# The first load of a decode attention kernel comes in two pieces: 16 rows, then 112

## The chip, the core and the metric

The kernel runs on one core of a Trainium2 chip. The metric is the device time of one execution in microseconds; less is better. The figures given for the kernel before are the median of three runs and one execution taken with the hardware profiler.

## What is computed

One decode step of a block with grouped-query attention over a long cache, gated by a small dense network. There are two sequences (B = 2) with one new token each, 32 query heads, 8 key/value heads, a cache of 32,768 positions, heads of 128, a model width of 512, and everything is float32. Cut to what matters:

```python
xn = layernorm(x)                                  # x: (2, 1, 512)
q  = (xn @ wq) split into 32 heads                 # wq: 512 x 4096
s  = softmax(q . k_cache / sqrt(128)) . v_cache    # both caches: 2 x 8 x 32768 x 128
s  = s @ wo                                        # wo: 4096 x 512
h  = relu(xn @ w1 + b1)**2                         # w1: 512 x 1792
g  = silu(h @ w2 + b2)                             # w2: 1792 x 512
return x + s * g
```

The two caches are 537 MB of the 561 MB that the kernel reads; each byte is used once.

## The kernel before

The host packs the inputs so that each load is a rectangle of 128 rows (one for each partition of the on-chip memory) with long contiguous rows. There are three large buffers of 128 x 64 KiB: `kslot`, `vslot` and `wbuf`. The sixteen pairs of a sequence and a key/value head are each cut in two halves of 16,384 positions, which makes 32 turns (`NT`). A turn takes one load of keys (`kt`, 8 MiB, into `kslot`) and one of values (`vt`, 8 MiB, into `vslot`).

All large loads are issued from SP, in an order written out by hand. At the head there are three, with nothing to wait for:

- L85: `wm`, the weights of the dense network (w1 and w2), 128 rows of 57,344 bytes, into the first 28/32 of `vslot`; it signals `gv`
- L87: `wq`, 128 rows of 65,536 bytes, into `wbuf`; it signals `wq_sem`
- L88: the first keys into `kslot`; it signals `gs`

Two small loads with x and the biases (`xr`, 16 KB, L126, and `x16`, 4 KB, L128) are issued from ACT.

Then PE makes three passes with one and the same body, `pe_values` (64 matmuls in the trace, two for each of the 32 in the code, L364: rows of `vslot` against the columns of `pT`), before the turns begin. The first multiplies by w1 and the second by w2, both out of `vslot`; the third is the product with wq, which ACT and DVE copy from `wbuf` into `vslot` (L200, L206, L209). Each pass starts when the semaphore `gv` has reached a count, 17 for each pass; 16 of the first 17 come from the load of `wm` and one from DVE:

```python
    dve.wait(t_pad)                                    # L164
    v.tensor_copy(pT[:, 0:128]..., xs[...]).then_inc(gv, 1)   # L165, L166
```

Ahead of these lines DVE makes the layer norm of x out of the small load (from L139) and fills the rest of `pT` (L163). The empty columns of `vslot` above `WM` are set to zero by GpSimd; `t_pad` stands for this. After the first pass, DVE goes on at L182 with what PE has turned (L374).

After the third pass SP issues the first load of values (L227, `vslot`). From there on each buffer is loaded again as soon as PE has used it: SP waits for the scores of a turn (L347) and issues the next keys (L237), then for its values (L364) and issues the next values (L240; the last one in two parts, L242 and L243). Once the turns are over, `wo` is loaded in seven pieces (`sp_last`, L326), and the last products, the gate and the sum with x follow (L392 to L432), then one store of 64 KB (L434). At the end SP clears all the semaphores used in one range (L435, L436).

Of the kernel before, what the change touches and what calls it, by code (L numbers as in the profile page):

```python
# [14 lines left out]
P = 128  # L15
# [13 lines left out]
WM = 28 * W  # L29
# [26 lines left out]
def build(nc, xr, x16, kt, vt, wq, wm, wo, out):  # L56
    pe, act, dve, pool, sp = (Engine(nc, e, n) for e, n in (
        (nc.tensor, "pe"), (nc.scalar, "act"), (nc.vector, "dve"), (nc.gpsimd, "pool"), (nc.sync, "sp")))
# [3 lines left out]
    def sb(name, *shape):  # L62
        return nc.alloc_sbuf_tensor(name, [P, *shape], F32)

    kslot, vslot, wbuf = sb("kslot", SLOT), sb("vslot", SLOT), sb("wbuf", SLOT)
# [3 lines left out]
    xb, gate, yb, gpad = sb("xb", P), sb("gate", P), sb("yb", P), sb("gpad", P)  # L69
# [10 lines left out]

    gv, ge, gb, gc, gd, gs, dm, ex, os, vh = (nc.alloc_semaphore(n) for n in ("gv", "ge", "gb", "gc", "gd", "gs", "dm", "ex", "os", "vh"))
    tail_sem = [nc.alloc_semaphore(f"tail{i}") for i in range(len(TAIL))]
    wq_sem, xr_sem, xb_sem, wx_sem, out_sem = (nc.alloc_semaphore(n) for n in ("wq", "xr", "xb", "wx", "out"))

    nc.sync.dma_start(vslot[:, 0:WM], wm[:, 0:WM]).then_inc(gv, 16)  # L85
    nc.sync.sem_clear(out_sem)
    nc.sync.dma_start(wbuf[:, :], wq).then_inc(wq_sem, 16)  # L87
    nc.sync.dma_start(kslot[:, :], kt[0, 0]).then_inc(gs, 16)  # L88
# [30 lines left out]
    t_pad = pool.done(g.memset(vslot[:, WM:], 0.0))  # L119
# [41 lines left out]
        t_x = dve.done(v.tensor_copy(xs[32 * q:32 * q + 32, :, :], xq[:, q, :, 0:8]))  # L161
    dve.wait(t_x, t_pT)
    v.tensor_copy(pT[:, 0:256].rearrange("p (d q z) -> p d q z", d=ND, q=4)[:, :, 0:3, 0:B], xs[:, :, None, 0:B].to_broadcast([P, ND, 3, B])).then_inc(gs, 17 * (PRO - 1) + 1)  # L163
    dve.wait(t_pad)  # L164
    v.tensor_copy(pT[:, 0:128].rearrange("p (h z) -> p h z", h=2)[:, :, 48:52].rearrange("p h (e b) -> p h e b", e=2),  # L165
                  xs[:, :, 0:B].rearrange("p (h e) b -> p h e b", h=2)).then_inc(gv, 1)  # L166

# [264 lines left out]
    t = dve.done(v.tensor_add(xb[:, :], yb[:, :], xb[:, :]))  # L432
    sp.wait(t)
    nc.sync.dma_start(out, xb[:, :]).then_inc(out_sem, 16)  # L434
    used = sorted(x.num for x in [e.sem for e in (pe, act, dve, pool, sp)] + [gv, ge, gb, gc, gd, gs, dm, ex, os, vh] + tail_sem + [wq_sem, xr_sem, xb_sem, wx_sem])  # L435
    nc.sync.sem_clear(range(used[0], used[-1] + 1))  # L436
    nc.sync.wait_ge(out_sem, 16)

# [44 lines left out]
```

## Time and profile before

| | us |
|---|---|
| median of the runs | 1302.14 |
| lowest and highest of the runs | 1302.06, 1302.2 |
| span of the profiled execution, first to last instruction | 1300.8 |
| PE busy | 691.4 |
| DVE busy | 86.0 |
| ACT busy | 99.1 |
| mean rate of the DMA engines over the span | 431 GB/s |

The profiled execution has no time of its own apart from its span, which is 1.34 us below the median of the runs; the difference lies before the first and after the last instruction. A row of the timeline or of the chain begins with the start in us from the beginning of the span and with the duration or the busy time of the group; `L85` is line 85 of the kernel; `x64` a count of instructions; and what stands in brackets is the idle time of the engine before, and what ended it. `SPq` and `ACTq` mark the instructions that issue transfers from those two engines; a row of them tells how long the issue took, not the transfer. In a list of transfers the last number of a row is the median time in us from issue to landing.

### The profile page before, as it was taken

To read this page: it belongs to the slowest core of one execution; us is meant where nothing else is said; L and a number is where in the kernel's file an instruction comes from. 1 tells how busy PE (TensorE), PEld (TensorE's weight loads), DVE (VectorE), ACT (ScalarE), POOL (GpSimd) and SP (SyncE) were. 2 spreads that over 40 slices of the span, in tenths; PEclk is the share of its full clock that TensorE was granted. 3 is DMA by queue.
4 is the path that set the end of the run, shared out by engine and by line. 5 is a ranking of instruction groups with operands and counts; after the bars stand their busy time and mean duration, and the time that the engine had idled before them with its cause. 6 is when DMAs were issued, how large, how long until landed. Compare 5 with 4: busy or idle time off the path is not lost.

```text
span 1300.8 us, 11201 instructions
## 1 busy us (share of the span) xinstructions
PE 691.4 (53%) x4781; PEld 189.5 (15%) x4781; DVE 86.0 (7%) x366; ACT 99.1 (8%) x202; POOL 5.7 (0%) x22
## 2 busy tenths in 40 slices
PE   3746546545545545645544644654554554554557
PEld 0111111111111111111111111111111111111112
DVE  2100000000000000000000000000000000000001
ACT  0301001010010001001010100001001000100100
POOL 1000000000000000000000000000000000000000
PEclk9877677677778677767767767767767767776878
DMA  9999999999999999999999999999999999999998
GB/s 420 419 451 419 447 423 429 441 419 451 419 451 419 451 419 431 439 419 451 419 451 419 451 419 431 439 419 451 419 451 419 451 419 431 439 419 451 419 435 373
DMA packets 10840, 561.08 MB, mean 431 GB/s; under 512 B 1216, under 2 KB 1368, under 8 KB 1752
## 3 DMA queue, kind: packets, MB, share of 16 engines
q1 hardware_dynamic: 10800, 561.06, 99.8%
q10 hardware_dynamic: 40, 0.02, 0.0%
HBM read 561.01 MB, written 0.07 MB: 431 GB/s over the span
## 4 chain that ended last, share of the span: by engine, by line
DMA 74%; PE 24%; issue 1%; DVE 0%; POOL 0%; SPq 0%; POOLq 0%
DMA vslot<-in_vt 70%; PE o_ps L364 24%; DMA wbuf<-in_wo 3%; DMA vslot<-in_wm 1%; PE wb L392 0%; DVE vslot L209 0%; DVE vslot L206 0%; PE acc L422 0%; POOL pT L197 0%; POOL pT L179 0%; SPq L243 0%; PE acc L426 0%; SPq L242 0%; DVE yb L430 0%; DVE xb L432 0%
## 5 line engine op out<-in xcount | busy, mean ns | idle before, releaser
L364 PE MATMUL o_ps<-vslot,pT 128*16 128x512 f32 x2304 | 327.6, 732 | 225.7 <-DMA vslot<-in_vt 201.5
L347 PE MATMUL sc<-kslot,qz 128*32 128x512 f32 x2048 | 294.1, 739 | 277.1 <-DMA kslot<-in_kt 277.1
L347 PEld LDWEIGHTS sc<-kslot,qz 128*32 128x32 f32 x2048 | 71.2, 132 | 478.5 <-DMA kslot<-in_kt 284.7
L364 PEld LDWEIGHTS o_ps<-vslot,pT 128*16 128x16 f32 x2304 | 69.6, 112 | 454.6 <-issue 223.5
L309 ACT ACTIVATE prob<-sc,nm 128x512 f32<-128x512 f32 x32 | 22.0, 687 | 633.9 <-DVE nm L277 633.9
L270 DVE TENSOR_REDUCE r<-sc 128x1 f32<-128x512 f32 x32 | 22.1, 692 | 557.7 <-PE sc L347 557.7
L318 ACT COPY o_sb<-o_ps 128x512 f32<-128x512 f32 x32 | 18.8, 586 | 480.2 <-PE o_ps L364 480.2
L353 PE MATMUL tp<-ident,prob 128*128 128x128 f32 x128 | 25.6, 333 | 50.7 <-ACT prob L309 50.7
L291 DVE TENSOR_REDUCE t<-ot 128x4 f32<-128x64 f32 x32 | 7.2, 225 | 547.6 <-PE ot L374 547.6
L374 PE MATMUL ot<-ident,o_sb 128*128 128x128 f32 x140 | 23.0, 287 | 25.0 <-ACT o_sb L318 22.9
L353 PEld LDWEIGHTS tp<-ident,prob 128*128 128x128 f32 x128 | 16.4, 164 | 56.8 <-ACT prob L309 56.8
L350 PE MATMUL ms<-ident,r 128*128 128x128 f32 x32 | 10.3, 323 | 26.4 <-DVE r L270 26.4
L374 PEld LDWEIGHTS ot<-ident,o_sb 128*128 128x128 f32 x140 | 14.7, 140 | 57.3 <-ACT o_sb L318 52.4
L311 ACT COPY pT<-tp 128x512 f32<-128x512 f32 x32 | 18.8, 586 | 28.4 <-PE tp L353 28.4
L309 ACT ACT_TABLE_LOAD x16 | 20.5, 1283 | 0.3
L350 PEld LDWEIGHTS ms<-ident,r 128*128 128x128 f32 x32 | 4.2, 133 | 55.4 <-DVE r L270 55.4
L355 PEld LDWEIGHTS ms<-selh,l 128*128 128x128 f32 x64 | 12.1, 236 | 0.0
L355 PE MATMUL ms<-selh,l 128*128 128x4 f32 x64 | 10.5, 235 | 0.0
L273 DVE TENSOR_REDUCE mh<-ms 128x4 f32<-128x128 f32 x32 | 9.3, 292 | 10.9 <-PE ms L350 10.9
L200 ACT COPY vslot<-wbuf 128x4096 f32<-128x4096 f32 x2 | 7.1, 3610 | 0.0
L309 ACT ACTIVATION_READ_ACCUMULATOR prob<-sc,nm 128x1 f32 x32 | 6.2, 192 | 0.0
L392 PE MATMUL wb<-wbuf,oX 128*16 128x512 f32 x24 | 4.4, 900 | 2.2 <-DMA wbuf<-in_wo 2.2
(86 smaller groups left out, 78.0 us busy)
## 6 DMA issues: line engine op xcount, KB each, us to landing
vslot<-in_vt SPq DMA_DIRECT2D x2, 4096.0 KB, 24.0
vslot<-in_wm SPq DMA_DIRECT2D x1, 7168.0 KB, 19.4
wbuf<-in_wo SPq DMA_DIRECT2D x1, 3072.0 KB, 34.9
vslot<-in_wo SPq DMA_DIRECT2D x1, 2048.0 KB, 13.6
vslot<-in_wo SPq DMA_DIRECT2D x2, 1024.0 KB, 12.0
kslot<-in_kt SPq DMA_DIRECT2D x32, 29.4
wbuf<-in_wo SPq DMA_DIRECT2D x1, 512.0 KB, 13.9
wbuf<-in_wo SPq DMA_DIRECT2D x2, 256.0 KB, 14.2
```

What stands on the lines that cost most here:

```text
L270: v.tensor_reduce(r1[:, :], sc[:, :], axis=AX.X, op=ALU.max).then_inc(dm, 1)
L273: did(f"mh{u}", v.tensor_reduce(mh[:, u, :], ms[:, :P].rearrange("p (a h) -> p h a", h=REP), axis=AX.X, op=ALU.max))
L291: did(f"t4{u}", v.tensor_reduce(t4[:, u, :], ot[:, :].rearrange("p (i y e) -> p e i y", i=4, y=NG)[:, :REP], axis=AX.XY, op=ALU.add))
L309: nc.scalar.activation(prob[:, :], sc[:, :], AF.Exp, bias=nm[:, u:u + 1], scale=SCALE, accum_out=l1[:, :]).then_inc(ex, 1)
L311: copy(pT[:, :], tp[:, :]).then_inc(gv, 1)
L318: copy(o_sb[:, :], o_ps[:, :]).then_inc(os, 1)
L347: ins = mm(sc[32 * c:32 * c + 32, :], qz[:, 28 - 4 * j:60 - 4 * j], kslot[:, lo:lo + W], start=(j == 0), stop=(j == NJ - 1))
L350: tr(ms[:, :P], r1[:, :].to_broadcast([P, P]), ident[:, :]).then_inc(pe.sem, 1)
L353: ins = tr(tp[:, k * P:(k + 1) * P], prob[:, k * P:(k + 1) * P], ident[:, :])
L355: mm(ms[:, :REP], l1[:, :].to_broadcast([P, P]), selh[:, :], start=True, stop=True).then_inc(pe.sem, 1)
L364: ins = mm(o_ps[32 * y:32 * y + 16, :], pT[:, 16 * n:16 * n + 16], vslot[:, n * W:(n + 1) * W], start=(n < NG), stop=(n >= 32 - NG))
L374: ins = tr(ot[:, lo:lo + P], o_sb[:, n * DH:(n + 1) * DH], ident[:, :])
```

## The change

The load of `wm` is issued as two transfers in place of one. The first has rows 0 to 15 of the 128, the second rows 16 to 127; the rows have the same 57,344 bytes as before. The second keeps the semaphore `gv`, on which the passes of PE count. The first has a semaphore of its own, `wm_sem`, and DVE waits for it ahead of the copy that completes the count of the first pass, so that this pass still starts only after all 128 rows are there. The new semaphore also enters the range that is cleared at the end.

```diff
-    wq_sem, xr_sem, xb_sem, wx_sem, out_sem = (nc.alloc_semaphore(n) for n in ("wq", "xr", "xb", "wx", "out"))
+    wq_sem, xr_sem, xb_sem, wx_sem, wm_sem, out_sem = (nc.alloc_semaphore(n) for n in ("wq", "xr", "xb", "wx", "wm", "out"))
 
-    nc.sync.dma_start(vslot[:, 0:WM], wm[:, 0:WM]).then_inc(gv, 16)
+    nc.sync.dma_start(vslot[0:16, 0:WM], wm[0:16, 0:WM]).then_inc(wm_sem, 16)
+    nc.sync.dma_start(vslot[16:P, 0:WM], wm[16:P, 0:WM]).then_inc(gv, 16)
     nc.sync.sem_clear(out_sem)
     nc.sync.dma_start(wbuf[:, :], wq).then_inc(wq_sem, 16)
     nc.sync.dma_start(kslot[:, :], kt[0, 0]).then_inc(gs, 16)
...
-    dve.wait(t_pad)
+    dve.wait(t_pad, (wm_sem, 16))
     v.tensor_copy(pT[:, 0:128].rearrange("p (h z) -> p h z", h=2)[:, :, 48:52].rearrange("p h (e b) -> p h e b", e=2),
                   xs[:, :, 0:B].rearrange("p (h e) b -> p h e b", h=2)).then_inc(gv, 1)
...
-    used = sorted(x.num for x in [e.sem for e in (pe, act, dve, pool, sp)] + [gv, ge, gb, gc, gd, gs, dm, ex, os, vh] + tail_sem + [wq_sem, xr_sem, xb_sem, wx_sem])
+    used = sorted(x.num for x in [e.sem for e in (pe, act, dve, pool, sp)] + [gv, ge, gb, gc, gd, gs, dm, ex, os, vh] + tail_sem + [wq_sem, xr_sem, xb_sem, wx_sem, wm_sem])
```

## The prediction

> **What bounds the kernel now.** I read the page's shares and DMA line first, then the chain that ended last, then the timeline of the first 70 us with the landings of the loads issued there, because the change touches nothing later.
>
> ```profile
> span 1300.8 us, 11201 instructions
> PE 691.4 (53%) x4781; PEld 189.5 (15%) x4781; DVE 86.0 (7%) x366; ACT 99.1 (8%) x202; POOL 5.7 (0%) x22
> DMA  9999999999999999999999999999999999999998
> DMA packets 10840, 561.08 MB, mean 431 GB/s; under 512 B 1216, under 2 KB 1368, under 8 KB 1752
> DMA 74%; PE 24%; issue 1%; DVE 0%; POOL 0%; SPq 0%; POOLq 0%
> ```
>
> No compute engine is busy much over half the span, and the 16 DMA engines are busy in every slice. The 24% of PE in the chain looks like a second bound. The merged chain in order of time shows that it is not:
>
> ```profile
> 0.74 19.42 DMA vslot<-in_wm
> 20.20 10.05 PE o_ps L364 x64
> 52.39 26.05 DMA vslot<-in_vt
> 78.43 0.04 issue
> ...
> 1162.04 0.04 issue
> 1200.74 0.04 issue
> 1239.44 0.04 issue
> ```
>
> The V loads land at 78.43, ..., 1162.04, 1200.74 and 1239.44: 30 steps in 1161.01 us, 38.70 us each, and the last two steps, 1200.74 - 1162.04 and 1239.44 - 1200.74, are 38.70 as well. A step moves one K and one V load of 8 MiB (128 rows of 65,536 B), 16.78 MB, so 433.5 GB/s, 27.1 GB/s for each of 16 engines, from beginning to end. The PE pieces of the chain lie inside the transfer of the next load, as the head of the timeline shows:
>
> ```profile
> 0.74 0.37 SPq L85 DMA_DIRECT2D vslot<-in_wm  x1
> 1.23 0.35 SPq L87 DMA_DIRECT2D wbuf<-in_wq  x1
> 1.28 0.60 ACTq L126 DMA_DIRECT2D prob<-in_xr  x1
> 1.63 0.42 SPq L88 DMA_DIRECT2D kslot<-in_kt  x1
> 11.67 0.67 DVE L139 TENSOR_REDUCE st<-prob 2x1 f32<-2x512 f32 x1 [8.81 <-DMA prob<-in_xr]
> 17.21 0.18 DVE L163 COPY pT<-xs 128x24 f32<-128x24 f32 x1
> 17.30 0.17 DVE L165 COPY pT<-xs 128x8 f32<-128x8 f32 x1
> 20.20 10.00 PE L364 MATMUL o_ps<-vslot,pT 128*16 128x512 f32 x64 [20.20 <-DMA vslot<-in_wm]
> 31.61 0.18 DVE L182 TENSOR_TENSOR hv<-ot,xs 128x24 f32<-128x24 f32 x1 [14.15 <-PE ot L374]
> 52.39 0.33 SPq L227 DMA_DIRECT2D vslot<-in_vt  x1
> 59.09 9.34 PE L347 MATMUL sc<-kslot,qz 128*32 128x512 f32 x64 [5.40 <-DMA kslot<-in_kt]
> 68.50 0.33 SPq L237 DMA_DIRECT2D kslot<-in_kt  x1
> ```
>
> The first V load goes out at 52.39, while the first K load is still arriving (it releases PE at 59.09): 6.7 us of queued work are left. The next K load goes out at 68.50, 9.9 us before that V load lands at 78.43. So the queue never runs dry, and the time of this kernel is: when the stream starts, the bytes at 433.5 GB/s, and the short tail. A microsecond lost or won at the head is carried to the end undiminished, since nothing behind it waits for anything but the stream.
>
> The rate at the head, from the median times between issue and landing in the first 60 us:
>
> ```profile
> vslot<-in_wm SPq DMA_DIRECT2D x1, 7168.0 KB, 19.4
> wbuf<-in_wq SPq DMA_DIRECT2D x1, 38.3
> kslot<-in_kt SPq DMA_DIRECT2D x1, 57.4
> ```
>
> wm lands at 0.74 + 19.42 = 20.16, wq at 1.23 + 38.3 = 39.5, K at 1.63 + 57.4 = 59.0: 19.4 and 19.5 apart, against 19.35 for 8 MiB at the steady rate. Going from one transfer to the next therefore costs 0.1 us or less. wm itself, 128 rows of 57,344 B = 7.34 MB, needs 16.93 us at that rate and takes 19.42: 2.49 us are start and landing. One row on each engine is 16.93 / 8 = 2.12 us; I call this a row-time.
>
> **The change part by part.** Durations are those of the profiled execution, whose span is 1300.8; the median of the runs is 1302.14, 1.34 more. I add differences to the median.
>
> *One DMA instruction more on SP.* 0.37 us, by the row of L85, ahead of wq and K. They go out some 0.4 us later, at about 1.6 and 2.0, and their turn comes at about 18 and 38: hidden by more than 15 us. The next thing that SP does is L227 at 52.39, after a wait: nothing. The small load of x from ACT's queue isn't behind it. At the hand-over between the two pieces the 0.1 us above is an upper bound; I take 0.
>
> *An earlier start.* 16 rows to describe instead of 128. At most all of the 2.49 us could go; at worst the start is later by some of the extra 0.37. The only row near this is the DMA of 8 rows on ACT (L126), whose instruction took 0.60 us, no less than that of 128 rows: the count of rows doesn't make the issue long. I take -0.2, and -2.49 to +0.4 as ends.
>
> *A wait of DVE on the 16 rows (L164).* Behind it are L165 and then L182 at 31.61, which waits for PE anyway; the first pass at L364 waits for L165, but also for the other 112 rows, which are behind the 16 on every engine. 17.30 against 20.20 leaves 2.9 us where the 16 rows land last at about 20: 0, and 0.2 (one L165) at worst.
>
> *One semaphore more to allocate and clear at the end.* It is within one range clear: 0.
>
> *The rate of the two pieces.* This is the term that decides. Every large transfer whose rate the trace shows writes all 128 partitions, and so no row tells whether 27.1 GB/s is the limit of an engine or of the place that it writes to. Those two are the same thing while each engine has an eighth of a hundred and twenty-eight rows of its own. They part as soon as all 16 engines write to 16 neighbouring partitions at once. Let the 16 partitions lie behind g of 16 write paths of 27.1 GB/s each. The first piece then takes 16/g row-times instead of one. g = 16 gives 2.12 us and no loss. g = 2 (each path has eight neighbours) gives 16.93 and a loss of 14.8; that is also what a rate in proportion to the partitions would give, 16/128 of 433.5 GB/s. These are the ends. Which one is nearer can't be read from a row: the small load of x (16 KB to 8 partitions, issued at 1.28, used at 11.67) spends its 10.4 us in line behind rows of wm. Between the ends the doublings leave g = 8 and g = 4; I take 4, the one nearer to the proportional rate, because neighbouring partitions are likelier to share a path than distant ones: 4 row-times, 8.47 us, a loss of 6.35.
>
> [...]
>
> *The second piece.* Seven rows for each engine, beginning at partition 16. If the places are the limit, the order matters too: with seven rows in line for each engine, the borders of the engines' shares no longer fall on those of the paths, and at any moment some paths have two or three writers and others none. Best: no collision, 7 row-times as now, 0. Worst within this picture: each row meets another one throughout, 14 row-times, +14.8. I take half of that, 3.5 row-times, +7.4. The engines end it at unequal times; what counts is the last one, since every landing waits for all 16, and a late engine has no slack in which to catch up (it has work queued to the end).
>
> Sum: -0.2 + 0 + 6.35 + 7.4 = +13.6 us. Against the span 1314.4; against the median 1315.7 (+1.0%).
>
> The loss shifts everything together: wm, wq, K land later by the same amount, PE's three first passes begin later by it, and the margin of 6.7 us at L227 remains. The load of x also slips behind the slow first row, by up to 6.35: DVE's chain would end at 17.47 + 6.35 = 23.8, still ahead of the first pass, then at 20.2 + 13.6 = 33.8.
>
> **The rivals.**
>
> *The places aren't the limit (no change).* Each engine does 1 + 7 = 8 rows, as before. 1302.14 - 0.2 = 1301.9. If 112 rows were dealt out by eights to 14 engines, these would have 9 rows at most instead of 8: one row-time more, 1301.9 + 2.1 = 1304.0, still inside 0.2%. For it: the rate per engine is the same everywhere in the trace, as if it were the engine's own. Against it: the trace has no narrow load on which this could show. Also in this class: if the rows of a place always go to the engine of that place, in whatever pieces, the sums per engine are again unchanged. [...]
>
> *Faster.* The mechanism is the start of the first transfer: 0.74 to the first byte. It would have to win 2.60 us (0.2% of 1302.14, about what a measurement of this kernel can tell from no change), and all that isn't steady transfer in wm is 2.49, landing included. So even the whole prize gives 1299.65 and counts as no change. The point from which this case decides isn't reached.
>
> *Slower by much more.* If the 112 rows are dealt one by one in turn, all 16 engines write to 16 neighbouring partitions in every round. Then each of the eight rounds takes 4 row-times: 8 x 6.35 = 50.8 lost, 1352.7. For it: nothing in the profile; against it: a load of 128 rows dealt so would show that now, and it runs at the full rate. Only a rule that treats 128 rows apart leaves room for it.
>
> *The margin at L227 goes.* If x's load slipped past the 112 rows, the first pass would wait for DVE instead; from a slip of 2.9 us relative to wm on the pass is late, and from 2.9 + 6.7 = 9.6 on the stream has a hole. Since x stands in line on the same engines as wm, I see no such slip: 0.
>
> **How the numbers follow.** The forecast, both pieces held up by the places they write to, +6.1 to +18: 0.55. Own range 1308 to 1320: 6.35 - 0.2 with a second piece that costs nothing, to 6.35 - 0.2 + 5.6 row-times. A small loss (g = 8 and no collision in the second piece, 2.12 + some, over 2.6): 0.05. Much slower: 0.08. No change: 0.30, of which most is at 1301.5 to 1302.5. Faster by over 0.2%: 0.02. So slower 0.55 + 0.05 + 0.08 = 0.68, same 0.30, faster 0.02. The range has to take in the no-change case: 1301.5 to 1319 leaves out the much slower runs, the uppermost of the forecast and a few of the lowest, under 2 in 10.
>
> **What would show it.** In the changed kernel's timeline the first pass at L364 would begin at about 34 instead of 20.2, PE's first scores at about 73 instead of 59.1, and the V landings would remain 38.70 apart, so that all of the loss is made before 75 us. If the no-change case holds, the first pass begins within half a microsecond of 20.2. Right in the sum and wrong in the split: the 16 rows can be seen to land, by the DVE wait at L164 or the landing of their DMA, at about 0.74 + 2.5 + 8.5 = 11.7 under g = 4, at 5.3 if nothing is held up, and at about 20 under g = 2. A step longer than 38.70 after the head, or a hole of the DMA share at 55 us or later, would be a cause that I haven't got.

## Result and the profile after

The changed kernel takes 1320.74 us (median of four runs, 1320.54 to 1321.36) against 1302.10 before: a ratio of 1.0143, 95% interval 1.0131 to 1.0155. It is slower by 18.6 us. The direction and the place were forecast; the size, 13.6, was not, and the time lies 1.7 us above the stated range. The profiled execution took 1320.57 us, with a span of 1319.2.

The timeline of the head of the changed kernel (L86 is the second load; what stood at L86 and below before is one line further down):

```profile
0.74 0.38 SPq L85 DMA_DIRECT2D vslot<-in_wm  x1
1.17 0.41 SPq L86 DMA_DIRECT2D vslot<-in_wm  x1
21.63 0.68 DVE L140 TENSOR_REDUCE st<-prob 2x1 f32<-2x512 f32 x1 [18.76 <-DMA prob<-in_xr]
27.27 0.17 DVE L166 COPY pT<-xs 128x8 f32<-128x8 f32 x1
39.04 9.49 PE L365 MATMUL o_ps<-vslot,pT 128*16 128x512 f32 x64 [39.04 <-DMA vslot<-in_wm]
69.98 0.33 SPq L228 DMA_DIRECT2D vslot<-in_vt  x1
77.73 8.93 PE L348 MATMUL sc<-kslot,qz 128*32 128x512 f32 x64 [6.45 <-DMA kslot<-in_kt]
```

The first pass begins at 39.04 in place of 20.20, 18.84 later; the first V load goes out 17.59 later and the first scores begin 18.64 later. Nothing is added after that. In the chain in order of time the K landings keep their step:

```profile
116.39 0.04 issue
...
1238.67 0.04 issue
1277.38 0.04 issue
```

From 116.39 to 1277.38 there are 30 steps of 38.70 us, the step of before. The whole loss is made inside the first 40 us, in the load of `wm`. Its two parts land as follows (list of transfers in the first 75 us; the size in KB where the list gives it, then the us from issue to landing):

```profile
vslot<-in_wm SPq DMA_DIRECT2D x1, 6272.0 KB, 37.8
vslot<-in_wm SPq DMA_DIRECT2D x1, 896.0 KB, 10.7
wbuf<-in_wq SPq DMA_DIRECT2D x1, 56.6
kslot<-in_kt SPq DMA_DIRECT2D x1, 75.6
```

The 16 rows are there at 0.74 + 10.7 = 11.4, the 112 rows at 1.17 + 37.8 = 39.0. So the 16 rows did what the prediction said of them (11.7 for four write paths), and the 112 rows took about 27.6 us instead of 14.8.

### The profile page after: what moved, and what is told of

The parts are those of the page before. It is cut to its first block, busy times and chain, and to the rows that moved or that the text cites. A ratio compares the mean times of both kernels' runs of the same rounds, so it can differ in the third digit from the quotient of the medians.

```text
span 1319.2 us, 11203 instructions
## 1 busy us (share of the span) xinstructions
PE 699.7 (53%) x4781; PEld 193.0 (15%) x4781; DVE 86.0 (7%) x366; ACT 99.1 (8%) x202; POOL 5.7 (0%) x22
## 2 busy tenths in 40 slices
DMA packets 10856, 561.08 MB, mean 425 GB/s; under 512 B 1232, under 2 KB 1384, under 8 KB 1768
## 4 chain that ended last, share of the span: by engine, by line
DMA 73%; PE 25%; issue 1%; another core or an unknown queue 0%; DVE 0%; ACT 0%; SPq 0%; POOL 0%; POOLq 0%
DMA kslot<-in_kt 69%; PE sc L348 23%; DMA vslot<-in_wm 3%; PE o_ps L365 2%; DMA wbuf<-in_wo 1%; DVE vslot L207 0%; PE acc L423 0%; PE tp L354 0%; SPq L327 0%; DVE r L271 0%; PE ot L375 0%; ACT pT L312 0%; ACT o_sb L176 0%; POOL pT L198 0%
## 5 line engine op out<-in xcount | busy, mean ns | idle before, releaser
L348 PE MATMUL sc<-kslot,qz 128*32 128x512 f32 x2048 | 298.3, 748 | 275.3 <-DMA kslot<-in_kt 275.3
L312 ACT COPY pT<-tp 128x512 f32<-128x512 f32 x32 | 18.8, 586 | 30.7 <-PE tp L354 30.7
L314 ACT COPY lh<-ms 128x4 f32<-128x4 f32 x32 | 5.4, 168 | 0.0
## 6 DMA issues: line engine op xcount, KB each, us to landing
vslot<-in_wm SPq DMA_DIRECT2D x1, 6272.0 KB, 37.8
vslot<-in_wm SPq DMA_DIRECT2D x1, 896.0 KB, 10.7
```

Source lines behind the costliest of these rows:

```text
L312: copy(pT[:, :], tp[:, :]).then_inc(gv, 1)
L348: ins = mm(sc[32 * c:32 * c + 32, :], qz[:, 28 - 4 * j:60 - 4 * j], kslot[:, lo:lo + W], start=(j == 0), stop=(j == NJ - 1))
```

## Experiments

All of them change only how `wm` is brought in, and DVE's wait for it. The times to compare with are those of the kernel before on the same chips, 1302.05 to 1302.23. The first of these kernels was run ten times, each of the others once. The four runs of the change lie up to 0.8 us apart, so a difference of that size between single runs means nothing. Except in the last two kernels, every load has a number of rows that divides by 16, and in the traces the packets of `wm` come sixteen at a time; "round" below means one such group, a row of 57,344 bytes on each of the 16 DMA engines, 2.12 us at the full rate.

### Is it the second transfer, or the partitions?

```diff
-    nc.sync.dma_start(vslot[0:16, 0:WM], wm[0:16, 0:WM]).then_inc(wm_sem, 16)
-    nc.sync.dma_start(vslot[16:P, 0:WM], wm[16:P, 0:WM]).then_inc(gv, 16)
+    C = 7 * W // 2
+    nc.sync.dma_start(vslot[:, 0:C], wm[:, 0:C]).then_inc(wm_sem, 16)
+    nc.sync.dma_start(vslot[:, C:WM], wm[:, C:WM]).then_inc(gv, 16)
```

> wm in two loads again, but cut by columns: all 128 rows of the first 1,792 columns, then all 128 rows of the other 12,544. If the loss comes from the places written to (few neighbouring partitions at a time), both loads are as wide as before: no loss, 1302.1 within 0.5, first pass at 20.2. If it comes from having two loads in place of one, the loss stays: about 1320.7, first pass at 39.

Measured: 1302.08, ratio 1.0008, interval 0.9991 to 1.0026. Nine of the ten runs lie between 1301.85 and 1302.80, the tenth at 1312.91; it makes the interval wide and puts the ratio above 1. The timeline:

```profile
20.24 8.47 PE L366 MATMUL o_ps<-vslot,pT 128*16 128x512 f32 x64 [20.24 <-DMA vslot<-in_wm]
58.94 9.61 PE L349 MATMUL sc<-kslot,qz 128*32 128x512 f32 x64 [7.95 <-DMA kslot<-in_kt]
```

Two transfers of the same two sizes cost nothing when both are 128 partitions wide: the first pass begins 0.04 us later than before, the scores 0.15 us earlier. This kernel says nothing on an earlier start with only 16 rows to describe, since its first load has 128; the trace of the change does. Its first packets of `wm` begin between 1.7 and 1.8 us of the span, as they do in the trace before.

### Neighbours against partitions eight apart

Eight loads of 16 rows each; only the choice of the 16 differs. Each of the three kernels has one of these lines in its loop (the end of the line, with the semaphores, is left out here):

```diff
+    for r in range(8):
+        nc.sync.dma_start(vslot[16 * r:16 * r + 16, 0:WM], wm[16 * r:16 * r + 16, 0:WM])...   # neighbours
+        nc.sync.dma_start(vslot[r:P:8, 0:WM], wm[r:P:8, 0:WM])...                             # eight apart
+        nc.sync.dma_start(vslot[r:P:8, 0:WM], wm[16 * r:16 * r + 16, 0:WM])...                # crossed
```

> wm in eight loads of 16 neighbouring rows each. If 16 neighbouring partitions have four write paths, each load takes 4 row-times: 8 x 8.47 = 67.7 us in place of 16.9, first pass at about 71, 1302.1 + 50.8 = 1352.9. If the loss is one per additional load of 0.5 us or less, under 1306. If rate goes with the share of partitions, 8 x 16.9 = 135 us, 1421.

> wm in eight loads of 16 rows each, every eighth row (0, 8, ..., 120, then 1, 9, ...). If neighbouring partitions share a path by fours, with 32 groups on 16 paths, 16 rows eight apart fall on at least 8 paths: 2 row-times each, 33.9 us for wm, first pass at about 37, 1302.1 + 16.9 = 1319.0; with a path for each group 1302 to 1303. If small loads as such are slow, as slow as eight loads of neighbouring rows, 1352.9.

> Eight loads of 16 rows: the source rows are neighbours (16 r to 16 r + 15), the destination partitions are eight apart (r, r + 8, ...). The weights so stand in other partitions than they should; only the time is of interest. If the destination decides, as eight loads with both sides eight apart: 1319 (or 1302 to 1303). If the source decides (neighbouring rows in HBM held up in one channel), as eight loads of neighbouring rows: 1352.9.

Measured: 1349.28 for neighbours, 1320.87 for eight apart, 1320.65 for the crossed one. The first pass in the three timelines, in this order:

```profile
67.67 9.13 PE L365 MATMUL o_ps<-vslot,pT 128*16 128x512 f32 x64 [67.67 <-DMA vslot<-in_wm]
```

```profile
39.13 9.38 PE L365 MATMUL o_ps<-vslot,pT 128*16 128x512 f32 x64 [39.13 <-DMA vslot<-in_wm]
```

```profile
39.09 9.50 PE L365 MATMUL o_ps<-vslot,pT 128*16 128x512 f32 x64 [39.09 <-DMA vslot<-in_wm]
```

Against 20.20 for eight rounds at the full rate, neighbours lose 47.47 us, 5.93 a round (8.05 in place of 2.12), and rows eight apart lose 18.93, 2.37 a round (4.48). In row-times of 2.12 us that is 3.8 and 2.1 a round. With paths of 27.1 GB/s, as in the prediction, these are the times of about four paths for 16 neighbours, and of about eight for 16 rows eight apart; this is an estimate from the two rounds, since no trace names a path. The expected 1352.9 and 1319.0 were a few us off, because a round took 3.8 and 2.1 row-times, not 4 and 2. The crossed kernel has the neighbours on the side of HBM and the wide spacing on the side of the chip's memory, and its time is that of the wide spacing (1320.65 beside 1320.87): here it is the place written to that counts, not the place read from.

### How 112 rows are shared out

Within the change, the 16 neighbours thus account for 5.9 of the 18.6 us. The other 12.7 are the 112 rows. This kernel replaces their one load by seven loads of 16 rows, each with every seventh row (seven lines in the kernel, written here as one):

```diff
-    nc.sync.dma_start(vslot[16:P, 0:WM], wm[16:P, 0:WM]).then_inc(gv, 16)
+    # r = 0 ... 6, the last one on gv
+    nc.sync.dma_start(vslot[16 + r:P:7, 0:WM], wm[16 + r:P:7, 0:WM]).then_inc(wm_sem, 16)
```

> As the change, but with the load of 112 rows cut into seven loads of 16 rows, every seventh row (16, 23, ..., 121; then 17, 24, ...). If a load of 112 rows is dealt to the engines in runs of seven, these are just the seven rounds that the engines go through in the change, and the time is the same within 0.5 us: 1320.7, first pass at 39.0. If 112 rows are dealt otherwise, it differs by microseconds: with dealing one by one in turn the change would be 16 neighbours a round, and this kernel faster than it.

Measured: 1321.48, 0.74 above the change and a little more than the 0.5 allowed for, with the first pass at 39.66, 0.6 us later, after six more issues on SP. A difference of that size is within what single runs of the change differ by, and the time alone would prove little. The stronger evidence is the course of the seven rounds. The windows below are cut where the packets of a round begin in the changed kernel, and a packet counts where it begins; the last number is the rate in GB/s. The changed kernel first, then the seven loads:

```profile
8.20:13.50 5.30, 0.00 (x0) 0.00 (x0) 0.00 (x0) 0.00 (x0) 0.00 (x0) 1.00 0.89 173
13.50:17.70 4.20, 0.00 (x0) 0.00 (x0) 0.00 (x0) 0.00 (x0) 0.00 (x0) 1.00 1.00 220
17.70:20.50 2.80, 0.00 (x0) 0.00 (x0) 0.00 (x0) 0.00 (x0) 0.00 (x0) 1.00 0.99 330
20.50:23.80 3.30, 0.00 (x0) 0.00 (x0) 2.03 (x5) 0.00 (x0) 0.00 (x0) 1.00 1.01 278
23.80:27.30 3.50, 0.00 (x0) 0.00 (x0) 2.90 (x11) 0.20 (x1) 0.00 (x0) 1.00 1.12 263
27.30:31.50 4.20, 0.00 (x0) 0.00 (x0) 0.14 (x2) 0.00 (x0) 0.00 (x0) 1.00 0.98 218
31.50:35.59 4.09, 0.00 (x0) 0.00 (x0) 0.00 (x0) 0.00 (x0) 0.00 (x0) 1.00 0.96 224
```

```profile
8.20:13.50 5.30, 0.00 (x0) 0.00 (x0) 1.95 (x4) 0.00 (x0) 0.00 (x0) 1.00 0.92 176
13.50:17.70 4.20, 0.00 (x0) 0.00 (x0) 3.03 (x11) 0.20 (x1) 0.00 (x0) 1.00 0.98 219
17.70:20.50 2.80, 0.00 (x0) 0.00 (x0) 0.00 (x0) 0.00 (x0) 0.00 (x0) 1.00 0.97 307
20.50:23.80 3.30, 0.00 (x0) 0.00 (x0) 0.00 (x0) 0.00 (x0) 0.00 (x0) 1.00 1.06 295
23.80:27.30 3.50, 0.00 (x0) 0.00 (x0) 0.00 (x0) 0.00 (x0) 0.00 (x0) 1.00 1.09 246
27.30:31.50 4.20, 0.00 (x0) 0.00 (x0) 0.00 (x0) 0.00 (x0) 0.00 (x0) 1.00 0.99 218
31.50:35.59 4.09, 0.00 (x0) 0.00 (x0) 0.12 (x1) 0.00 (x0) 0.00 (x0) 1.00 0.98 224
```

The rounds of the one load of 112 rows have the same fast and slow places in the same order as seven loads in which I chose the rows. The rates differ by 23 GB/s at most in any window (330 and 307). So the 112 rows go as if an engine got seven neighbouring rows, one after the other, and the 16 engines wrote in each round to partitions seven apart. That is inferred from the match, since the trace doesn't name the engine of a row. The profile's count agrees that both parts use all 16 engines: 16 small packets more than before (1232 under 512 B in place of 1216).

### The partition at which a load begins

If each engine gets a run of neighbouring rows, the partition at which a load begins may matter as well as the number of its rows. Two kernels set the one against the other.

```diff
+    nc.sync.dma_start(vslot[0:64, 0:WM], wm[0:64, 0:WM]).then_inc(wm_sem, 16)       # two halves
+    nc.sync.dma_start(vslot[64:128, 0:WM], wm[64:128, 0:WM]).then_inc(gv, 16)
...
+    nc.sync.dma_start(vslot[32:96, 0:WM], wm[32:96, 0:WM]).then_inc(wm_sem, 16)     # the middle first
+    nc.sync.dma_start(vslot[0:32, 0:WM], wm[0:32, 0:WM]).then_inc(wm_sem, 16)
+    nc.sync.dma_start(vslot[96:P, 0:WM], wm[96:P, 0:WM]).then_inc(gv, 16)
```

> wm in two loads of 64 rows, 0 to 63 and 64 to 127. [...] Then in each half two engines write to each of 8 paths: 8 rounds at the 4.46 us measured for two writers, 35.7 us for wm in place of 16.9, about 1320.9, first pass at 39. If the rows were dealt one by one in turn (row r to engine r mod 16), every round would write 16 neighbours, 8 x 8.03, about 1349. If 64 rows are enough to keep the engines apart: 1302.

> wm in three loads: rows 32 to 95, then 0 to 31, then 96 to 127. The same theory: in runs of four from partition 32 on, each engine has a path of its own, so the first load of 64 rows goes at the full rate, 4 x 2.12 = 8.5 us, landing about 11 us after its issue, where 64 rows from partition 0 need 17.8 (landing at about 20). The two loads of 32 rows (runs of two, two writers on each path) take 8.9 each. Sum 26.3 against 16.9: 1302.1 + 9.4 = 1311.5, first pass at 29.6. If it is only the number of rows in a load that matters, the first load lands after 20 us and the sum is as in two loads of 64: 1320.9.

Measured: 1321.05 for two halves, with the first pass at 39.31; 1311.95 for the middle first, with the first pass at 30.20 (forecast 1311.5 and 29.6). The landings and the rate of the middle one:

```profile
vslot<-in_wm SPq DMA_DIRECT2D x1, 3584.0 KB, 12.2
vslot<-in_wm SPq DMA_DIRECT2D x2, 1792.0 KB, 24.1
```

```profile
5.40:11.80 6.40, 0.00 (x0) 0.00 (x0) 1.79 (x4) 0.00 (x0) 0.00 (x0) 1.00 1.30 432
```

Sixty-four rows from partition 32 go at 432 GB/s, the full rate; loads of 64 from 0 and from 64 go at about half, since together they take 19.1 us longer than the 16.9 of the undivided load, 36.0 us or 4.5 a round. Three loads beat two by 9 us, with the fast load of 64 rows among them: where a load begins counts, not its number of rows alone.

Both forecasts were added up from the author's assumption on which engines share a path, and no run shows a path or the engine of a row. The runs show times in its place: 2.12 us a round for 64 rows from partition 32, 4.5 for the two halves, and for the first pass of the middle one a delay of 10.0 us (30.20 against 20.20), with 9.4 worked out.

### The same change the other way round

```diff
+    nc.sync.dma_start(vslot[0:112, 0:WM], wm[0:112, 0:WM]).then_inc(wm_sem, 16)
+    nc.sync.dma_start(vslot[112:128, 0:WM], wm[112:128, 0:WM]).then_inc(gv, 16)
```

> The change in the other order and place: rows 0 to 111 first, then rows 112 to 127. If the loss is the sum of 16 neighbours (5.9 us) and of runs of seven that collide (12.7), whatever the partition they start at, then 1302.1 + 18.6 = 1320.7 within 1.5. If the 112 rows only lose time because the narrow load ahead of them leaves the engines out of step, they keep the full rate here: 5.9 alone, 1308.

Measured: 1321.08. The 112 rows land 30.7 us after their issue when nothing stands ahead of them (all 128 in one load: 19.4), so they aren't slowed by engines that the 16 rows have left out of step; they are slow by themselves.

### Who is held up by a shared path

A shared path could hold up the engines that share it and no others, or all 16. The prediction took the first for granted. Two kernels tell these apart: their first load has 64 rows, like the one from partition 32 that went at 432 GB/s, and begins eight or four rows lower:

```diff
+    nc.sync.dma_start(vslot[s:s + 64, 0:WM], wm[s:s + 64, 0:WM]).then_inc(wm_sem, 16)    # s = 24, s = 28
+    nc.sync.dma_start(vslot[0:s, 0:WM], wm[0:s, 0:WM]).then_inc(wm_sem, 16)
+    nc.sync.dma_start(vslot[s + 64:P, 0:WM], wm[s + 64:P, 0:WM]).then_inc(gv, 16)
```

> wm in three loads: rows 24 to 87 first, then 0 to 23, then 88 to 127. [...] If a shared path holds up all engines, every round takes 4.1 to 4.5 us for all 16: 205 to 222 GB/s from 3 to 20 us. [...] The sum is worked out only for the first load, since the other two use fewer engines.

> wm in three loads: rows 28 to 91 first, then 0 to 27, then 92 to 127. [...] If any shared path holds up all: 205 to 222 GB/s until 20 us. If it takes two shared paths, as in the rounds of the change with 14 paths used (218 to 224 GB/s) against the one with 15 (330): above 300 GB/s here and 205 to 222 with rows 24 to 87.

Measured, the rate over three rounds of the first load, from partition 24 and then from 28:

```profile
5.90:19.40 13.50, 0.00 (x0) 0.00 (x0) 2.35 (x5) 0.00 (x0) 0.00 (x0) 1.00 1.01 205
```

```profile
4.80:11.45 6.65, 0.00 (x0) 0.00 (x0) 0.00 (x0) 0.00 (x0) 0.42 (x2) 1.00 1.04 399
```

From 28 the rate is 399 GB/s, nearly the 432 of the load from 32; from 24 it is 205. The duration of each packet, which the traces also hold, tells more, without any choice of windows. From partition 28, 14 packets of the second round took 2.12 to 2.18 us and two took 4.33 and 4.39: one pair goes at half speed, as if it shared a path, and leaves the other 14 engines nearly alone. From partition 24, all 16 took 4.49 to 4.54: every engine goes at half speed. The rates are those of the last outcome written down for 28, above 300 GB/s there and 205 to 222 from 24. The 14 and 15 paths in it are the author's estimate, which no run counts: the two slow packets fit one pair on a path from 28, four rows lower than 32, and from 24, eight rows lower, two pairs are taken by doubling that.

Both patterns are also in the changed kernel's rounds where they can be kept apart. In the second round (220 GB/s) all 16 packets took 4.11 to 4.25 us; in the third (330) 14 took 2.40 to 2.77 and two 4.05 and 4.08. These two are then late, and the rounds overlap: the fourth reached 278, and the fifth 263 before the last two fell back to 218 and 224.

The whole kernels took 1337.20 and 1329.94. Their other loads (24 and 40 rows, 28 and 36) don't divide by 16; their packets come in twelves and tens, and in fourteens and twelves, so fewer engines share them, and their times aren't worked out here. Why all 16 engines are held up from 24 and only two from 28, the runs don't show; it stays open.

## Why the prediction was right in direction and wrong in size

*The bound and the carrying-through: right.* A loss at the head was forecast to pass undiminished to the end, and 18.84 us at the first pass became 18.64 at the first scores and 18.4 in the span. The margin at the first V load remained: issued at 69.98, with the K load arriving until 77.7.

*SP's extra issue, DVE's extra wait, the semaphore, the load of x: right that they cost nothing.* L86 took 0.41 us. L166 ended at 27.44 and the first pass waited until 39.04. The load of x came in 10.0 us later, more than the 6.35 allowed for, and still lay well inside.

*An earlier start: -0.2 was too hopeful.* The first packets begin between 1.7 and 1.8 us with 16 rows in the first load as with 128: 0.

*The 16 rows: right.* Forecast 6.35 lost with g = 4; measured 5.93 for a round of 16 neighbours. The two ends (0 and 14.8) are excluded. That paths are behind it was not shown; shown is the round of 3.8 row-times. The choice of 4 over 8 was a guess between two values with no row behind it, so part of this is luck.

*The 112 rows: the step that failed.* Without a row for it I took half of the worst case, 3.5 row-times, +7.4. It cost about 12.7: six row-times of the worst case's seven. The idea of seven rows in line for each engine fits the runs: round by round the load goes like seven loads of every seventh row. That two engines then write to some paths and none to others was an estimate; shown are a round in which all 16 packets took 4.11 to 4.25 us and one in which 14 took 2.40 to 2.77. What failed is that a shared path was taken to slow its own users only: in the slow rounds of the change, and in every round measured from partition 24 (205 GB/s), all 16 engines went at about half speed. The half itself was a guess with no row behind it. 5.93 + 12.7 = 18.6. The upper end of the range was cut at 1319.0 although the forecast case's own reached 1320 and the worst in that picture 1323; the cut was made to save width, not from a row.

*The rivals.* "The places aren't the limit" and "faster" are refuted. "Slower by much more" needed dealing one by one in turn; the rounds of the change go like runs instead, and eight loads of neighbours, which act out that rival, took 1349.28 where 1352.7 was worked out.

## What to carry to other kernels

Where the DMA stream is the bound, cut a load by columns and keep all 128 partitions in each piece: that was free here (1302.08 us), and cutting it by rows cost 19 us for the most natural cuts (16 + 112, 64 + 64, 112 + 16). If rows must be cut, measure where a piece begins as well as its size: 64 rows went at 432 GB/s from partition 32, at 399 from 28 and at 205 from 24. "One row for each engine" doesn't make a piece fast (16 neighbours took 8.05 us in place of 2.12), and what is left when a narrow piece is taken off can be slow too: 112 rows took 27.6 us for 14.8 us of work.

## What the runs showed of the hardware

- Sixteen neighbouring partitions take 8.05 us a round, 16 that are eight apart 4.48, 64 from partition 32 on 2.12 (432 GB/s). If the first two are four and two writers on a path, as estimated above, four get 28.5 GB/s together (4 x 57,344 B in 8.05 us) and two only 25.6.
- Sixty-four rows from partition 28 go at 399 GB/s, with two of the 16 packets of a round at 4.33 and 4.39 us and 14 at 2.12 to 2.18; from partition 24 they go at 205 GB/s, with all 16 at 4.49 to 4.54.
- A load of 112 rows goes through the same rounds as if it were dealt to the engines in runs of seven. How a load of 128 rows is dealt was not shown: it runs at the full rate, 2.12 us a round, and no run here names the engine of a row.
